# Key features made half by half, a changed warm-up, and weight stages at other key steps, in an attention and two-layer feed-forward kernel

## The chip, the cores and the metric

One core of a Trainium2 chip. The metric is device time in microseconds (us) of one execution, lower is better. The engines are TensorE (PE, with its weight loads as PEld), VectorE (DVE), ScalarE (ACT), GpSimd (POOL) and SyncE (SP, which issues DMAs here). Each works through its own queue in order.

## What is computed

Linear attention with random features over 4 batches, 8 heads, 576 positions and 64 dimensions, and then two feed-forward layers on the 2304 tokens (512 to 2048 and back):

```python
def phi(x):
    proj = np.einsum('bhsd,md->bhsm', x, omega)
    sq = np.sum(x * x, axis=-1, keepdims=True) / 2.0
    h = proj - sq
    h = h - np.max(h, axis=-1, keepdims=True)
    return np.exp(h) / np.sqrt(m)
q_p, k_p = (phi(q_s), phi(k_s))
kv = np.einsum('bhsm,bhsd->bhmd', k_p, v)
z = np.sum(k_p, axis=2)
...
g = np.maximum(h, 0.0) + alpha * np.minimum(h, 0.0)   # layer 1; layer 2 squares max(h, 0)
return (g @ w_out).astype(np.float32)
```

## The kernel before, in words

Every engine's order is the order in which the program is written out; a semaphore is waited for wherever an instruction uses what another engine has made. The work falls into three stretches: the keys (to about 57 us), the queries (to about 140 us), and the two feed-forward layers.

The keys come in 18 tiles of 128 tokens. `k_step(i)` (L656) issues, in this order: the load of a coming tile (SP), the products of key features and values of tile i-3 (`kv_part`, L644, PE), the projections of tile i (`project`, L598, 16 matmuls into one of two PSUM tiles of two banks), its square sums (`square_sums`, L605, into columns 0 to 7 of `tt[i % 2]`, a PSUM tile of one bank), and then for tile i-1 the maximum over features (`greatest`, L611, DVE), the bias made from it and the square sums (`bias`, L617 and L618, DVE), and the exponentials (`feature`, L623, ACT, eight activations). `kv_place` (L650, DVE) copies a finished batch out of PSUM. POOL copies values (L688) and squares the next tile (L587). Projections of tile i use the PSUM tile that the features of tile i-2 have read.

`idle(n)` (L589 to L592) issues n matmuls of zeros, 504 columns wide, into columns 8 to 511 of `tt[1]`; their results are not used. `ZEROS` gives how many stand ahead of the first projection, between the first projection and its square sums, and behind the square sums of tile 1.

Weights of the feed-forward layers are decoded and split beside this by `made()`, a generator; each `onward` does one stage. The first unit's stages 0 to 10 (L335 to L345) are: scale the first half's high words (ACT, L138); its low words (ACT, L143); shift it (DVE, L157) and scale the second half's high words; merge it (DVE L163, POOL L165) and the second's low words; shift the second; merge the second and cast (ACT, L244); remainder (DVE, L247); cast; remainder; two sums (DVE, L179); two sums. Stage 11 is empty for this unit. The loop at L771 runs one stage behind each key step from `MAKE_K` on, but none behind step `PLACED`; the two steps that follow run one each, and from query step 3 on `upto` counts stages.

The tiles `mx` and `nb` of a step come from a pool of four buffers.

Of the kernel before, what the change touches and what calls it, by code (L numbers as in the profile page):

```python
# [9 lines left out]
F32 = mybir.dt.float32  # L10
# [9 lines left out]
P = 128  # L20
B, H, S, D = 4, 8, 576, 64
T = B * S
NT = T // P
NP = H // 2
# [10 lines left out]
HB = NB // 2  # L35
NPAIR = NF // 2
QW = 2 * P
MAKE_K = 5

PLACED = 11  # L40

ZEROS = (8, 4, 4)

HELD = 5

# [16 lines left out]
def tile_performer_moe(ctx, tc, qt, kt, qn, kn, vn, omt, w1i, w1o, al, w2i, w2o, out):  # L62
    nc = tc.nc
# [378 lines left out]
    def onward(most, blk):  # L442

        ask(most, blk)
        next(making[0])
# [6 lines left out]
    def ask(most, blk):  # L452

        limit[0], room[0] = most, blk
        if not making:
            making.append(made())
            next(making[0])
        fetches[0]()
# [75 lines left out]
    def attention():  # L534
        with ExitStack() as ac:
# [3 lines left out]
            sm = ac.enter_context(tc.tile_pool(name="sm", bufs=4, side="right"))  # L539
# [8 lines left out]
            tt = [po.tile([P, 512], F32, name=f"t{j}") for j in range(2)]  # L548

            def projections(i):  # L550

                return (pb, pa)[i % 2].tile([P, 2, NP, M], F32, name="h")
# [23 lines left out]
            def load(key):  # L576
                which, i = key
                raws[key] = raw = ld.tile([P, NP, P], F32, name="raw")
                nc.sync.dma_start(out=raw, in_=(kt if which == "k" else qt)[i])

            def load_values(i):
                vls[i] = kp.tile([P, H, D], F32, name="vr", bufs=4)
                nc.sync.dma_start(out=vls[i], in_=vn[i * P:(i + 1) * P])

            def square(key):
                sqts[key] = wk.tile([P, NP, P], F32, name="sqt", bufs=2)
                nc.gpsimd.tensor_tensor(out=sqts[key], in0=raws[key], in1=raws[key], op=ALU.mult)  # L587

            def idle(n):  # L589

                for _ in range(n):
                    nc.tensor.matmul(tt[1][:, H:], zeros[:, 0:P], zeros[:, H:], start=True, stop=True)  # L592

            def project(key, pj):

                for c in range(NP):
                    for j, rows in enumerate(HALVES):
                        nc.tensor.matmul(pj[:, j, c, :], raws[key][rows, c, :], om[rows], start=True, stop=True)  # L598

            def square_sums(key, o):  # L600

                sqt = sqts.pop(key)
                for c in range(NP):
                    for rows in HALVES:
                        nc.tensor.matmul(o[rows, 2 * c:2 * c + 2], sqt[:, c, rows], pick,  # L605
                                         start=True, stop=True, skip_group_check=True)
                return o.rearrange("p (c j) -> p j c", j=2)

            def greatest(pj):
                mx = sm.tile([P, 2, NP], F32, name="mx")  # L610
                nc.vector.reduce_max(out=mx, in_=pj, axis=AX.X)  # L611
                return mx

            def bias(mx, nsq):

                nb = sm.tile([P, 2, NP], F32, name="nb")
                nc.vector.tensor_tensor(out=mx, in0=nsq, in1=mx, op=ALU.add)  # L617
                nc.vector.tensor_tensor(out=nb, in0=nsq, in1=mx, op=ALU.subtract)  # L618
                return nb

            def feature(pj, nb, e):
                for c in range(NP):
                    nc.scalar.activation(out=e[:, c, :], in_=pj[:, c, :], func=AF.Exp, bias=nb[:, c:c + 1])  # L623

            def parts_of(i):

                t0, out = i * P, []
                while t0 < (i + 1) * P:
                    t1 = min((i + 1) * P, (t0 // S + 1) * S)
                    out.append((t0 // S, slice(t0 - i * P, t1 - i * P), t0 % S == 0, t1 % S == 0))  # L630
                    t0 = t1
                return out


            pjs, nsqs, es, acc = {}, {}, {}, {}

            def kv_part(i, part):
                b, rs, first, last = part
                if first:
                    acc[b] = products()  # L640
                for h in range(H):
                    g, k = divmod(h, G)
                    for ms in HALVES:
                        nc.tensor.matmul(  # L644
                            acc[b][ms, g, k * W:(k + 1) * W], es[i][rs, h % 2, h // 2, ms], vas[i % 4][rs, h],
                            start=first and k == 0, stop=last, skip_group_check=True)

            def kv_place(b):
                o = acc.pop(b)
                nc.vector.tensor_copy(out=kvr[:, b].rearrange("p (g h) w -> p g (h w)", g=NG), in_=o[:, :, 0:G * W])  # L650
# [5 lines left out]
            def k_step(i):  # L656
                if 0 <= i < NT:
                    k = next(ahead, None)
                    if k:
                        load(k)  # L660
                    if i + 1 < NT:
                        load_values(i + 1)
                todo = parts_of(i - 3) if has(i - 3) else []
                placed = []
                if todo:
                    kv_part(i - 3, todo[0])
                    placed = [b for b, _, _, last in todo if last]
                if has(i):
                    pjs[i] = projections(i)
                    project(("k", i), pjs[i])  # L670
                    if i == 0:
                        idle(ZEROS[1])
                    nsqs[i] = square_sums(("k", i), tt[i % 2][:, 0:H])
                    if i == 1:
                        idle(ZEROS[2])
                if has(i - 1):
                    pj = pjs.pop(i - 1)
                    nb = bias(greatest(pj), nsqs.pop(i - 1))
                    es[i - 1] = e = kp.tile([P, 2, NP, M], F32, name="e", bufs=4)
                    feature(pj[:, 0], nb[:, 0], e[:, 0])  # L680
                for b in placed:
                    kv_place(b)
                if has(i - 1):
                    feature(pj[:, 1], nb[:, 1], e[:, 1])
                if len(todo) > 1:
                    kv_part(i - 3, todo[1])
                if has(i - 1):
                    nc.gpsimd.tensor_copy(out=vas[(i - 1) % 4][:, :, 0:D], in_=vls.pop(i - 1))  # L688
                if has(i + 1):
                    square(("k", i + 1))  # L690
                es.pop(i - 3, None)
# [4 lines left out]
            def q_step(s, make=lambda: None, more=lambda: None):  # L696
# [31 lines left out]
                if has(s):  # L728
                    qpj[s] = projections(s)
                    project(("q", s), qpj[s])  # L730
                    mx = greatest(qpj[s])
# [9 lines left out]
                if has(s):  # L741
                    nsq = square_sums(("q", s), tt[s % 2 if s < 2 else 1][:, 0:H])
                    qnb[s] = bias(mx, nsq)
# [13 lines left out]
            zeros = ka.tile([P, 512], mybir.dt.bfloat16, name="zeros")  # L757
            nc.vector.memset(zeros, 0.0)
            nc.vector.memset(warm, 0.0)
            for rows, queue in zip(HALVES, (nc.sync, nc.scalar)):  # L760
                queue.dma_start(out=om[rows], in_=omt)
            nc.scalar.activation(out=warm, in_=warm, func=AF.Exp)
            idle(ZEROS[0])
            load(next(ahead))
            load(next(ahead))
            k_step(-1)
            constants()
            nc.vector.tensor_scalar(out=om, in0=om, scalar1=scale, scalar2=None, op0=ALU.mult)
            load(next(ahead))
            load_values(0)  # L770
            for i in range(NT):  # L771
                k_step(i)
                if i == 1:
                    ask(1, BLOCKS - 1)
                elif i >= MAKE_K and i != PLACED:
                    onward(1, BLOCKS - 1)
                if i == 3:
                    gate[0] = 4
                    ask(1, BLOCKS - 1)
                if i == 2:  # L780
                    nc.sync.dma_start(out=al_sb, in_=al)
                if i == 8:
                    nc.vector.tensor_scalar(out=sg_sb, in0=al_sb, scalar1=1.0, scalar2=-2.0, op0=ALU.is_gt, op1=ALU.mult)
                    nc.vector.tensor_scalar(out=sg_sb, in0=sg_sb, scalar1=1.0, scalar2=None, op0=ALU.add)
                if i == NT - 1:
                    square(("q", 0))
# [272 lines left out]
    COMPLETE = {6: (0,), 7: (1, 2), 8: (3,), 9: (4, 5)}  # L1059

    attention()
    xp = ctx.enter_context(tc.tile_pool(name="xp", bufs=1, reuse_waits="tile"))
    for n in (T1, T2, T3):
# [23 lines left out]
    for n, (layer, k, turn, p) in enumerate(plan):  # L1087
# [12 lines left out]
        for m, got in enumerate(steps, DRAINED if n == 0 else 0):  # L1100
# [29 lines left out]
            for _ in range(FILL[0 if whole else 1][m]):  # L1130
                part, _ = next(fill, (None, None))
# [316 lines left out]
```

## Time and profile before

| | |
|---|---|
| median of 3 runs | 872.86 us (872.68 to 872.99) |
| the profiled execution | 872.57 us |
| its span | 870.8 us |
| PE busy | 865.3 us, 99% of the span |
| DVE busy | 676.0 us, 78% |
| ACT busy | 520.5 us, 60% |
| POOL busy | 96.8 us, 11% |

The span runs from the first instruction to the last; the rest of the execution's time lies around it. Matmuls are pipelined and their ends are modelled, so that PE's busy share overstates how close PE is to its limit; starts of matmuls and of weight loads are what to go by. In the rows below, a bracket at the end of a row is the idle time of that engine ahead of the row and what ended it.

### The profile page before, as it was taken

The numbers are of one execution on the slowest core, as the hardware profiler recorded it, in microseconds if no ns is written. First come the engines' busy times: TensorE is split into PE (matmuls) and PEld (weight loads), VectorE is DVE, ScalarE is ACT, GpSimd is POOL, SyncE is SP. The second block draws the span as 40 slices with busy tenths as digits, with TensorE's granted clock in tenths as the row PEclk, the third lists the DMA queues.
The fourth block names the chain that finished last, engine by engine and source line by source line (L and its number), as shares of the span: only waits on it lengthen the run. The fifth ranks groups of instructions, "written<-read, shape, count | busy, mean of one in ns | idle before, by whom it ended". The sixth has DMA issues, their size and how long they took to land.

```text
span 870.8 us, 17509 instructions
## 1 busy us (share of the span) xinstructions
PE 865.3 (99%) x6812; PEld 801.1 (92%) x6812; DVE 676.0 (78%) x1117; ACT 520.5 (60%) x1027; POOL 96.8 (11%) x138
## 2 busy tenths in 40 slices
PE   9999999999999999999999999999999999999998
PEld 7898889899999999989999999998899988999888
DVE  4778986998996776897877965669965699756686
ACT  5888886989876666577667733335423355333442
POOL 6652342111101000001000000000000000000000
PEclk9999999999999999999999999999999999999999
DMA  8545305899837999939999966777797686876774
GB/s 280 187 131 177 111 14 203 281 312 345 301 142 276 384 372 376 343 109 352 400 405 383 350 224 214 233 270 267 258 302 248 211 314 253 295 258 224 298 258 147
DMA packets 88530, 228.76 MB, mean 263 GB/s; under 512 B 6784, under 2 KB 19456, under 8 KB 83456
## 3 DMA queue, kind: packets, MB, share of 16 engines
q1 hardware_dynamic: 78880, 192.21, 61.5%
q0 software_dynamic: 9216, 33.56, 11.5%
q10 hardware_dynamic: 352, 1.87, 0.6%
q8 instruction: 54, 0.88, 0.4%
q14 instruction: 28, 0.23, 0.1%
HBM read 170.47 MB, written 57.15 MB: 261 GB/s over the span
## 4 chain that ended last, share of the span: by engine, by line
PE 97%; ACT 2%; issue 0%; DVE 0%; ACTq 0%
PE h L838 30%; PE y L1034 23%; PE sumc L1227 11%; PE spare L838 10%; PE suma L1227 9%; PE h L598 4%; PE o L644 2%; PE t L605 2%; PE t L718 2%; PE o L750 2%; PE t L737 1%; PE t L592 1%; ACT e L623 1%; PE h L1227 0%; ACT gh L863 0%
## 5 line engine op out<-in xcount | busy, mean ns | idle before, releaser
L838 PE MATMUL h<-xh,w 128*128 128x384 f32 x1016 | 286.3, 337 | 0.7 <-ACT s L863 0.4
L838 PEld LDWEIGHTS h<-xh,w 128*128 128x128 f32 x1016 | 186.3, 188 | 4.0 <-ACT s L863 0.7
L1034 PE MATMUL y<-gh,w 128*128 128x512 f32 (+1 forms) x768 | 174.0, 337 | 0.0
L838 PE MATMUL h<-xl,w 128*128 128x384 f32 x508 | 170.4, 335 | 0.0
L1034 PEld LDWEIGHTS y<-gh,w 128*128 128x128 f32 x768 | 130.8, 188 | 11.7
L1034 PE MATMUL y<-gl,w 128*128 128x512 f32 (+1 forms) x384 | 102.4, 337 | 0.0
L1242 ACT CAST gh<-g 128x768 fp32r<-128x768 f32 x72 | 56.9, 833 | 74.1 <-PE suma L1227 33.1
L838 PEld LDWEIGHTS h<-xl,w 128*128 128x128 f32 x508 | 95.5, 188 | 2.0
L838 PE MATMUL spare<-xh,w 128*128 128x384 f32 x336 | 91.4, 335 | 0.0
L1244 DVE TENSOR_TENSOR gl<-g,gh 128x768 fp32r<-128x768 f32 x72 | 65.7, 953 | 14.3 <-PE suma L1227 7.1
L1227 PE MATMUL sumc<-w,gh 128*128 128x512 f32 (+1 forms) x296 | 76.6, 379 | 0.0
L1034 PEld LDWEIGHTS y<-gl,w 128*128 128x128 f32 x384 | 67.1, 188 | 9.6
L838 PEld LDWEIGHTS spare<-xh,w 128*128 128x128 f32 x336 | 61.3, 188 | 0.5 <-DVE c L905 0.3
L1227 PEld LDWEIGHTS sumc<-w,gh 128*128 128x128 f32 x296 | 52.8, 189 | 9.3
L863 ACT ACTIVATE s<-h,sg_sb 128x384 f32<-128x384 f32 x66 | 38.1, 578 | 38.2 <-PE h L838 38.2
L611 DVE TENSOR_REDUCE mx<-h 128x8 f32<-128x1024 f32 x36 | 44.0, 1223 | 21.7 <-PE h L598 21.1
L881 DVE SCALAR_TENSOR_TENSOR c<-c,al_sb 128x768 f32<-128x768 f32 x48 | 49.2, 1025 | 10.2 <-ACT c L863 10.2
L838 PE MATMUL spare<-xl,w 128*128 128x384 f32 x168 | 56.2, 334 | 0.0
L876 DVE SCALAR_TENSOR_TENSOR c<-h,sg_sb,s 128x384 f32<-128x384 f32 x66 | 40.5, 614 | 18.3 <-PE h L838 7.2
L1227 PE MATMUL suma<-w,gh 128*128 128x512 f32 x216 | 52.4, 391 | 0.0
L1227 PE MATMUL sumc<-w,gl 128*128 128x256 f32 x280 | 48.5, 282 | 0.0
L887 DVE SCALAR_TENSOR_TENSOR gl<-c,sg_sb,gh 128x768 fp32r<-128x768 f32 x48 | 48.4, 1009 | 0.0
(133 smaller groups left out, 1484.7 us busy)
## 6 DMA issues: line engine op xcount, KB each, us to landing
w<-k SPq DMA_DIRECT2D x99, 512.0 KB, 5.2
w<-k SPq DMA_DIRECT2D x39, 1024.0 KB, 4.8
w<-k SPq DMA_DIRECT2D x26, 896.0 KB, 8.8
k<-ms SPq DMA_DIRECT2D x36, 512.0 KB, 7.7
k<-w SPq DMA_DIRECT2D x16, 512.0 KB, 6.2
x<-in_w2i POOLq DMA_DIRECT2D x16, 512.0 KB, 7.0
x<-in_w2o POOLq DMA_DIRECT2D x16, 512.0 KB, 7.2
ms<-in_w1o POOLq DMA_DIRECT2D x14, 512.0 KB, 5.7
```

The lines of the kernel that those rows point to most:

```text
L598: nc.tensor.matmul(pj[:, j, c, :], raws[key][rows, c, :], om[rows], start=True, stop=True)
L605: nc.tensor.matmul(o[rows, 2 * c:2 * c + 2], sqt[:, c, rows], pick, start=True, stop=True, skip_group_check=True)
L611: nc.vector.reduce_max(out=mx, in_=pj, axis=AX.X)
L838: nc.tensor.matmul(out, w[:, u, a, cs], tiles[v, b][:, kc], start=start and kc == 0 and j == 0, stop=stop and kc == 1 and j == 2, skip_gro ...
L863: nc.scalar.mul(out=to, in_=of, mul=sg_sb[:, 2 * p + i:2 * p + i + 1])
L876: nc.vector.scalar_tensor_tensor(out=c[:, ts], in0=b, scalar=sign, in1=s, op0=ALU.mult, op1=ALU.add)
L881: nc.vector.scalar_tensor_tensor(out=c, in0=c, scalar=slope, in1=c, op0=ALU.mult, op1=ALU.max)
L887: nc.vector.scalar_tensor_tensor(out=gl[:, i], in0=c, scalar=sign, in1=gh[:, i].bitcast(F32), op0=ALU.mult, op1=ALU.subtract)
L1034: nc.tensor.matmul(y[a0 // 512][:, a0 % 512:a0 % 512 + a1 - a0], u[:, i, c * P:(c + 1) * P], v[:, i, ts], start=first and j == 0 and a0 % ...
L1227: nc.tensor.matmul(to[c] if v == 3 or banks else to[c][:, :QW], (l if v == 2 else h)[:, r, c * P:(c + 1) * P], both(r) if v == 3 else w[:, ...
L1242: nc.scalar.copy(out=h[:, r], in_=f[:, r])
L1244: nc.vector.tensor_tensor(out=l[:, r], in0=f[:, r], in1=h[:, r].bitcast(F32), op=ALU.subtract)
```

## The change

Three things. `greatest` and `bias` are called once for each half of a key tile (4 of its 8 groups of 128 features), so that the order on DVE is maximum, two bias instructions, maximum, two bias instructions; `mx` and `nb` come from the same pool of four. The zeros between the first projection and its square sums are gone, and those behind the square sums of tile 1 are five instead of four and are written to `tt[0]` instead of `tt[1]`. And the first unit's twelve stages behind the key loop's steps run at the steps of a table.

```diff
-MAKE_K = 5
-
-PLACED = 11
-
-ZEROS = (8, 4, 4)
+MAKE_K = {5: 1, 7: 1, 9: 1, 10: 1, 12: 2, 13: 1, 14: 1, 15: 1, 16: 1, 17: 2}
+
+ZEROS = 8, 5
...
-            def idle(n):
+            def idle(n, j=1):
 
                 for _ in range(n):
-                    nc.tensor.matmul(tt[1][:, H:], zeros[:, 0:P], zeros[:, H:], start=True, stop=True)
+                    nc.tensor.matmul(tt[j][:, H:], zeros[:, 0:P], zeros[:, H:], start=True, stop=True)
...
-            def greatest(pj):
-                mx = sm.tile([P, 2, NP], F32, name="mx")
+            def greatest(pj, n=2):
+                mx = sm.tile([P, 2, NP], F32, name="mx")[:, :n]
                 nc.vector.reduce_max(out=mx, in_=pj, axis=AX.X)
                 return mx
 
-            def bias(mx, nsq):
-
-                nb = sm.tile([P, 2, NP], F32, name="nb")
+            def bias(mx, nsq, n=2):
+
+                nb = sm.tile([P, 2, NP], F32, name="nb")[:, :n]
...
                     project(("k", i), pjs[i])
-                    if i == 0:
-                        idle(ZEROS[1])
                     nsqs[i] = square_sums(("k", i), tt[i % 2][:, 0:H])
                     if i == 1:
-                        idle(ZEROS[2])
+                        idle(ZEROS[1], 0)
                 if has(i - 1):
                     pj = pjs.pop(i - 1)
-                    nb = bias(greatest(pj), nsqs.pop(i - 1))
                     es[i - 1] = e = kp.tile([P, 2, NP, M], F32, name="e", bufs=4)
-                    feature(pj[:, 0], nb[:, 0], e[:, 0])
+                    nsq = nsqs.pop(i - 1)
+                    nb = [bias(greatest(pj[:, j:j + 1], 1), nsq[:, j:j + 1], 1)[:, 0] for j in range(2)]
+                    feature(pj[:, 0], nb[0], e[:, 0])
                 for b in placed:
                     kv_place(b)
                 if has(i - 1):
-                    feature(pj[:, 1], nb[:, 1], e[:, 1])
+                    feature(pj[:, 1], nb[1], e[:, 1])
...
-                elif i >= MAKE_K and i != PLACED:
+                for _ in range(MAKE_K.get(i, 0)):
                     onward(1, BLOCKS - 1)
```

## Rows read from the trace of the kernel before

**Rows 1.** The page, busy time of each engine over the span, share, instructions.
```profile
PE 865.3 (99%) x6812; PEld 801.1 (92%) x6812; DVE 676.0 (78%) x1117; ACT 520.5 (60%) x1027; POOL 96.8 (11%) x138
```
**Rows 2.** The chain that ended last, 0 to 75 us: start, length, engine, line.
```profile
1.20 3.54 PE t L592 x8
4.73 1.55 PE h L598 x16
...
14.35 0.56 PE t L605 x16
14.91 0.99 PE o L644 x32
15.90 1.09 PE h L598 x16
...
36.89 2.18 ACT e L623 x8
```
**Rows 3.** The opening in order of time: start, length, engine, line, operation, tiles.
```profile
5.95 1.04 POOL L587 TENSOR_TENSOR sqt<-raw 128x512 f32<-128x512 f32 x1
...
7.86 0.17 DVE L617 TENSOR_TENSOR mx<-t,mx 128x8 f32<-128x8 f32 x1 [0.29 <-PE t L605]
...
8.06 0.17 DVE L618 TENSOR_TENSOR nb<-t,mx 128x8 f32<-128x8 f32 x1
...
8.32 2.17 ACT L623 ACTIVATE e<-h,nb 128x128 f32<-128x128 f32 x8 [5.45 <-DVE nb L618]
...
8.83 0.63 PE L605 MATMUL t<-pick,sqt 128*64 128x2 f32 x16
...
8.95 1.23 DVE L611 TENSOR_REDUCE mx<-h 128x8 f32<-128x1024 f32 x1 [0.72 <-PE h L598]
...
9.40 1.02 PE L592 MATMUL t<-zeros 128*128 128x504 bf16 x4
...
10.46 0.17 DVE L617 TENSOR_TENSOR mx<-t,mx 128x8 f32<-128x8 f32 x1 [0.28 <-PE t L592]
10.54 0.97 PEld L598 LDWEIGHTS h<-om,raw 64*128 64x128 f32 x16 [0.61 <-ACT e L623]
```
**Rows 4.** The same view, steady key steps.
```profile
15.83 1.16 PE L598 MATMUL h<-om,raw 64*128 64x128 f32 x16
...
17.04 1.22 DVE L611 TENSOR_REDUCE mx<-h 128x8 f32<-128x1024 f32 x1 [0.94 <-PE h L598]
...
18.64 0.17 DVE L618 TENSOR_TENSOR nb<-t,mx 128x8 f32<-128x8 f32 x1
...
18.90 2.17 ACT L623 ACTIVATE e<-h,nb 128x128 f32<-128x128 f32 x8 [0.54 <-DVE nb L618]
```
**Rows 5.** The same view, around the features that the chain names at 36.89.
```profile
36.10 0.97 PEld L598 LDWEIGHTS h<-om,raw 64*128 64x128 f32 x16
...
36.40 0.17 DVE L617 TENSOR_TENSOR mx<-t,mx 128x8 f32<-128x8 f32 x1 [0.51 <-PE o L644]
...
39.11 0.97 PEld L598 LDWEIGHTS h<-om,raw 64*128 64x128 f32 x16 [0.44 <-ACT e L623]
```
**Rows 6.** Groups by line and shape, 9 to 57 us: busy us, mean ns, idle before.
```profile
L611 DVE TENSOR_REDUCE mx<-h 128x8 f32<-128x1024 f32 x17 | 20.8, 1222 | 10.9 <-PE h L598 10.9
...
L650 DVE COPY kvr<-o 128x520 f32<-128x520 f32 x3 | 2.1, 689 | 0.0
...
L247 DVE TENSOR_TENSOR w<-wf,w 128x512 fp32r<-128x512 f32 x2 | 2.1, 1026 | 0.2 <-ACT w L244 0.2
...
L163 DVE SCALAR_TENSOR_TENSOR x<-x,t 128x512 int32<-128x512 int32 x2 | 1.4, 680 | 0.0
...
L157 DVE TENSOR_SCALAR t<-x 128x512 int32<-128x512 int32 x2 | 0.8, 421 | 0.0
```
**Rows 7.** Busy by stretch at the span's end: PE, PEld, DVE, ACT, POOL, granted clock.
```profile
869.00:870.80 1.80, 0.00 (x0) 0.00 (x0) 0.00 (x0) 0.00 (x0) 0.00 (x0) 1.00 0.21 73
```
**Rows 8.** Waits of PE, 56 to 165 us: total, times, longest.
```profile
PE h L838 <- ACT c L863: 0.3, 1, 0.3
```

## The prediction

> **What bounds the kernel now.** I read the engines' busy times first, then the chain that ended last, then the opening in order of time, then the groups by line. TensorE (PE) is busy for 99% of the span [rows 1]; as its ends are modelled, I don't take that for a bound by itself. The chain says more: from the third projection to 75 us it runs on PE, in steps of projection (1.09 us), square sums (0.56) and keys-times-values (0.99), 2.64 us together, and leaves PE at one long place, 36.89, for 2.18 us of ScalarE (ACT) features; in the opening the features of tile 0, at 8.32, hold up the third projection in the same way [rows 3]. So a key step is bound by PE, and what can be won in these steps is PE's waiting: 0.6 us ahead of the third projection (weight loads idle 0.61 at 10.54) [rows 3], and 0.37 us at 39.11 (39.11 less 36.10 is 3.01, a step is 2.64) [rows 5]. From 56 to 165 us PE waits for another engine once, 0.3 us [rows 8]. So what the key steps gain or lose moves everything behind them by the same amount; nothing later gives it back, as the later work is ordered behind it on the same engine.
>
> **How tight a step is.** A projection goes into one of two PSUM tiles, so projection i waits for the features of i-2. In the steady rows [rows 4]: projection at 15.83, maximum (L611) at 17.04, ACT at 18.90 and its features over 2.17 later, at 21.07. That loop is 5.24 us, with 0.05 to PE again 5.29, against two steps of PE, 5.28. VectorE (DVE) needs 17.04 to 18.64 and most of L618's 0.17, of which the next start overlaps a part (I count 0.08): 1.68 us of each 2.64.
>
> **Part 1: the opening.** Removed: the four zero matmuls between projection 0 and its square sums, about 1 us of PE (four take 1.02) [rows 3]. Projection 0 ends at 6.28 (4.73 and 1.55) [rows 2]. The square sums of 0 then end at 6.85; POOL squares tile 1 from 5.95 to 6.99 [rows 3], so the squares of 0 are done by then and tile 1 has landed. Projection 1 ends at 7.94, square sums 1 at 8.50. Five zeros follow; at 1.02 for four they take about 1.24 and end at 9.7.
>
> What matters is where these five write: tt[0], the tile in which the square sums of key tile 0 lie, and they come in program order ahead of bias 0, which reads those. In the kernel before, the zeros behind square sums 1 wrote tt[1], and the row of bias 1 (L617, 10.46) shows what that does: the maximum of 1 ended at 10.18, square sums 1 at 9.46, and still L617 started only 0.04 us behind the last zero matmul (9.40 and 1.02 give 10.42), which the row names as releaser [rows 3]. The columns are disjoint, the wait is there all the same. Bias 0, reading tt[0], has no such row: its L617 at 7.86 waited for the square sums alone. After the change the two change places: bias 1 is free of the zeros, and bias 0 gets them. Before, the wait cost 0.28 us of DVE, under cover of ACT's features of 0. Bias 0 has no cover: nothing else feeds ACT yet.
>
> Worked out: L617 at 9.74, L618 0.20 behind (7.86 to 8.06), ACT 0.26 behind that (8.06 to 8.32) [rows 3]: features begin at 10.20. Queued behind the waiting L617 on DVE is the second half's maximum: it begins 0.08 after L618, at 10.02, takes 0.69 (below), L617 and L618 follow, and the second four activations can begin at about 11.27; four take 1.17 (2.17 less four of 0.25), to 12.43, and 0.05 later projection 2 runs: 12.48 against 10.54, **+1.93** (+1.8 to +2.1 with the half maximum and the fifth zero at their bounds). PE waits from 9.7 to 12.5.
>
> **Part 2: halves.** No row shows a maximum over 512. The whole, 1024 values, takes 1.222; a DVE copy of 520 values out of PSUM takes 0.689, which puts a value at 1.06 ns and the fixed part at 0.14 us; half of the whole would be 0.61 [rows 6]. I take 0.69, as the copy is the same engine reading as many values from the same memory; bounds 0.61 and 0.72. The Trainium skill ("VectorE: DVE Perf Modes", section on the TRN2 errata) gives a PSUM-source instruction a fixed 120 cycles plus one per value at 0.96 GHz; an estimate from that page is 0.66, and 1.19 for the whole, where the trace has 1.22, so I keep the row's figure; by the page's the shortage below would be about a third smaller.
>
> One half then costs DVE 0.69, something from there to L618, and 0.08 to the next start. From the maximum's end to L618 it is 0.38 in the steady row (17.04 and 1.22 to 18.64) [rows 4]; L617 to L618 alone is 0.20 [rows 3]. I take 0.31, between them and nearer the steady row, as the second half has no square sums left to wait for. A step takes 2.17 (1.94 to 2.30), where it took 1.68. What it buys: ACT begins after one half, 1.25 instead of 1.86 us behind the projection, but the second half's bias gates the second four activations, so features end about 3.49 behind and the loop, with 1.21 ahead of the maximum and 0.05 behind the features, is 4.75, 0.53 shorter than two steps of PE. That lead removes no PE wait where there was none; it can cover one.
>
> **Part 3: weight stages.** The twelve stages that ran at key steps 5 to 10 and 12 to 17 run at 5, 7, 9, 10, 12 (two), 13 to 16 and 17 (two, the second empty). All are done by the same step, so the query steps keep theirs. No weight DMA moves: both transfers of the first unit are issued at steps 1 and 3, and SP's queue of key loads is passed by nothing. POOL's two merges (L165, an addition of the size of a squaring, 1.04) [rows 3] go from steps 8 and 10 to 10 and 12, in front of a copy and a squaring there; a tile is squared in the step before the one that uses it, so that 1.04 is under cover of most of a step's 2.64: nothing, and 1.04 at the worst, once a merge. ACT has one scaling or cast in a step at most, and 2.17 of features in 2.64; what it lacks it borrows from the lead.
>
> DVE is what runs short. Step 11 has the copy of kvr (0.69, so 0.61 to the next start), step 12 now has shift and merge (0.42 and 0.68, so 0.34 and 0.60), step 13 the remainder L247 (1.03, so 0.95) [rows 6]: with three steps of 2.17 that is 9.01, against 7.92 of PE. 1.09 too much, less the lead of 0.53: PE waits 0.56 at projection 14. Steps 14 to 17 hold 8.68, another remainder (0.85), a kvr copy and four sums (0.5 each by half a remainder, as they have half its elements, 1.8 in all with their overlap), 11.9 against PE's 11.7 (4 steps of 2.64 and 1.1 for the tile whose keys-times-values is issued in two parts), and ACT's cast at 14 finds the lead spent: about 0.35 more. **+0.9**; at 0.61 for a half it is 0, at 2.30 a step 0.13 more in each of seven, 1.8.
>
> The wait at 36.40 (L617 held 0.5 us, though what it reads was ready) cost PE 0.37 because the loop had no lead; step 11 is left with one: **-0.37** (0 if DVE's shortage meets it).
>
> **Sum.** 1.93 + 0.9 - 0.37 = 2.46 us on the profiled execution, 872.57 (span 870.8 and 1.77 around it): 875.03. The median of the runs is 0.29 above that execution: **875.3**.
>
> **Rivals.**
> *The zeros don't hold bias 0* (not slower). Then L617 follows the first half's maximum at 7.13, ACT begins at 7.59, its second half at 8.66, projection 2 runs at 9.87, 0.67 earlier than before; with +0.9 and -0.37 that is -0.14: 872.7. It decides at one point, whether the first L617 starts near 7.1 or near 9.7. For it: the columns are disjoint. Against it: the row of bias 1. Chance 0.10.
>
> *DVE doesn't run short.* With a half at 0.61 the shortage is covered by the lead: 1.93 - 0.37 = 1.56, 874.4. For it: the maximum may have no fixed part to speak of; against it the copies. Chance 0.12.
>
> *TensorE's clock falls in the new wait of 2.8 us.* The first eight zeros took 3.54 us, 0.44 each, against 0.25 in the later four, and projection 0 took 1.55 against 1.09 [rows 2, 3]: the lower of the two levels, 1.2 GHz, early on. One key step at the first pace instead of the second, 2.64 times 0.44 over 0.25, costs 2.0: 877.3. At the end of the span PE does nothing for at least 1.8 us and the granted clock stays at 1.00 [rows 7], which speaks against, though the new wait is longer. The Trainium skill ("TensorE: Matmul & The Clock Gate", section "Why this matters for your kernels") says that PE-idle gaps between bursts bring the clock down to half; the trace has no gap so long between bursts. Chance 0.14.
>
> *Faster by over 0.2%.* No hold and no shortage together give -0.67 - 0.37, 871.8; for less than 871.1 another 0.7 would have to come from a wait that these views don't show. Chance 0.02.
>
> **How the numbers follow.** The forecast has 0.62. About 0.2% (1.75 us, so 874.6) is what a measurement of this kernel can tell from no change. Slower: 0.55 of the forecast's 0.62, 0.03 of the second rival, 0.14: 0.72. Same: 0.07, 0.09 and the first rival's 0.10, together 0.26. Faster 0.02. The range 873.8 to 877.6 holds the forecast with its bounds (874.0 to 876.6), the second rival and over half of the clock's; it leaves out the first and the last.
>
> **What would show it.** Right: the first L617 at 9.7 released by L592, projection 2 at 12.5, DVE back to back over key steps 11 to 15 with PE waiting for features at projections 14 and 15. Wrong: L617 at 7.1; no wait of PE behind 36 us; key-step matmuls at half speed behind 12.5.

## The result, and the profile after

The changed kernel took 879.55 us (median of 9 runs, 878.97 to 882.53) and the kernel before, beside it, 872.68 (872.30 to 879.21). The ratio is 1.0077, 95% interval 1.0063 to 1.0091: slower by 6.9 us, where 2.4 were forecast, and outside the stated range, whose upper end was 877.6. The profiled execution of the changed kernel is the one at 882.53, its slowest, with a span of 880.8; a second profile of the same kernel (below, span 877.1, 878.88 us) is nearer to the median. The kernel before has some slow runs of its own, 7 of the 83 beside the experiments, at 875.4 to 879.2 us with a granted clock of 0.992 to 0.996 over the whole run, and they widen the intervals below.

The page after: span, busy times as in [rows 1], and TensorE's granted clock in 40 slices of 22 us, in tenths.

```profile
span 880.8 us, 17576 instructions
PE 871.0 (99%) x6809; PEld 807.1 (92%) x6809; DVE 682.2 (77%) x1171; ACT 520.8 (59%) x1027; POOL 97.1 (11%) x138
PEclk7899999999999999999999999999999999999999
```

PE is still "99% busy"; the line that tells is the clock, below full in the first two slices. The opening in order of time, as in [rows 3] (L590 is the zeros, L609 the maximum, L615 and L616 the bias, L621 the features, L596 the projection):

```profile
6.16 1.16 PE L596 MATMUL h<-om,raw 64*128 64x128 f32 x16
...
7.82 1.24 PE L590 MATMUL t<-zeros 128*128 128x504 bf16 x5
...
9.09 0.16 DVE L615 TENSOR_TENSOR mx<-t,mx 128x4 f32<-128x4 f32 x1 [2.69 <-PE t L590]
9.29 0.16 DVE L616 TENSOR_TENSOR nb<-t,mx 128x4 f32<-128x4 f32 x1
9.37 0.68 DVE L609 TENSOR_REDUCE mx<-h 128x4 f32<-128x512 f32 x1
...
10.15 4.25 ACT L621 ACTIVATE e<-h,nb 128x128 f32<-128x128 f32 x16 [7.27 <-DVE mx L609]
...
12.38 2.08 PE L596 MATMUL h<-om,raw 64*128 64x128 f32 x16 [3.32 <-ACT e L621]
...
17.17 2.08 PE L596 MATMUL h<-om,raw 64*128 64x128 f32 x16
```

Bias 0 waits for the five zeros, as forecast: 2.69 us of DVE, released by L590. ACT then starts not behind the first half's bias (9.29 and 0.16) but 0.10 us behind the end of the second half's maximum (9.37 and 0.68), which the row names. PE waits 3.32 us, and its projections then take 2.08 us and stand 4.79 us apart (12.38 to 17.17), not 1.16 as in [rows 4] and 2.64. From the start of projection 1 (6.16) to that of projection 2 it is 6.22 us; before, it was 2.81 (7.74 to 10.55). Busy time by stretch, columns as in [rows 7]:

```profile
5.00:10.00 5.00, 4.05 (x65) 2.94 (x63) 1.57 (x4) 0.00 (x0) 4.68 (x12) 1.00 1.03 377
10.00:15.00 5.00, 2.62 (x28) 2.40 (x30) 2.70 (x10) 4.25 (x16) 1.66 (x3) 0.61 0.81 286
15.00:20.00 5.00, 5.00 (x72) 4.66 (x72) 2.12 (x7) 2.18 (x8) 2.20 (x3) 0.50 0.57 177
20.00:25.00 5.00, 5.00 (x72) 4.66 (x73) 1.94 (x6) 2.18 (x8) 1.59 (x2) 0.50 0.41 140
25.00:30.00 5.00, 5.00 (x96) 4.75 (x96) 2.40 (x9) 2.73 (x9) 2.31 (x3) 0.68 0.48 114
```

The clock is at its lower level, 1.2 GHz (0.50), for three key steps and part of a fourth, with PE busy throughout. In the first 5 us of a span the column can't be used in this way: there it reads 1.00 in every profile, while the first eight zeros take some 0.44 us each [rows 2] and the five at 7.82 take 0.25; the pace tells. Behind the low stretch the clock is full, and DVE is what PE waits for by way of ACT:

```profile
51.65 1.17 DVE L245 TENSOR_TENSOR w<-wf,w 128x512 fp32r<-128x512 f32 x1
52.73 0.68 DVE L609 TENSOR_REDUCE mx<-h 128x4 f32<-128x512 f32 x1
...
53.61 1.16 PE L596 MATMUL h<-om,raw 64*128 64x128 f32 x16 [0.54 <-ACT e L621]
...
54.59 2.18 ACT L621 ACTIVATE e<-h,nb 128x128 f32<-128x128 f32 x8 [1.03 <-DVE mx L609]
...
56.82 1.16 PE L596 MATMUL h<-om,raw 64*128 64x128 f32 x16 [0.50 <-ACT e L621]
```

These two are projections 14 and 15.

Where the 10.0 us of span went, by the starts of projections in the two profiles. To projection 2: 12.38 against 10.55, +1.8. From there to projection 6: 30.06 less 12.38 is 17.68, against 21.12 less 10.55, +7.1 (the clock). From 6 to the first query tile: 66.02 less 30.06 is 35.96, against 56.23 less 21.12, +0.85 (DVE). The rest to the end, 814.8 against 814.6: +0.2. In the profile nearer to the median the same four are +2.3, +2.9, +0.85 and +0.2, 6.3 in all. The third of these is too small by a halt in the profile of before, which the prediction passed over: projection 6 takes 1.67 us there instead of 1.16, and the idle in it ends on nothing that the profile shows ("issue").

```profile
21.12 1.67 PE L598 MATMUL h<-om,raw 64*128 64x128 f32 x16
...
22.19 0.41 PEld L598 LDWEIGHTS h<-om,raw 64*128 64x128 f32 x5 [0.33 <-issue]
```

Without that 0.5 us, before would take 34.60 from projection 6 to the first query tile, and the change 1.36 more.

### The profile page after: what moved, and what is told of

It reads as the page before. It is cut to its first block, busy times and chain, and to the rows that moved or that the text cites. A ratio compares the mean times of both kernels' runs of the same rounds, so it can differ in the third digit from the quotient of the medians.

```text
span 880.8 us, 17576 instructions
## 1 busy us (share of the span) xinstructions
PE 871.0 (99%) x6809; PEld 807.1 (92%) x6809; DVE 682.2 (77%) x1171; ACT 520.8 (59%) x1027; POOL 97.1 (11%) x138
## 4 chain that ended last, share of the span: by engine, by line
PE 93%; ACT 3%; DVE 2%; issue 1%; DMA 0%; POOL 0%; DVEq 0%; ACTq 0%
PE h L835 28%; PE y L1031 22%; PE sumc L1224 11%; PE spare L835 10%; PE suma L1224 9%; PE h L596 4%; PE t L715 2%; PE t L603 2%; PE o L642 2%; PE o L747 2%; PE t L734 1%; DVE mx L609 1%; PE t L590 1%; ACT e L621 0%; DMA ms<-in_w1i 0%
## 5 line engine op out<-in xcount | busy, mean ns | idle before, releaser
L609 DVE TENSOR_REDUCE mx<-h 128x4 f32<-128x512 f32 (+1 forms) x54 | 46.7, 864 | 20.3 <-PE h L596 19.3
L621 ACT ACTIVATE e<-h,nb 128x128 f32<-128x128 f32 x144 | 39.2, 391 | 23.6 <-DVE mx L609 23.5
L596 PE MATMUL h<-om,raw 64*128 64x128 f32 x576 | 45.2, 300 | 4.6 <-ACT e L621 4.4
```

## The experiments

The kernel before took 872.77 us beside the first four runs, 872.58 beside the next four, 872.50 beside the last three; "above before" is against the one beside it. Two theories stood at the start. The first: the zeros in tt[0] hold bias 0, PE falls idle, and the clock falls with that. The rival: there are too few zeros, or the halves and the stages are what costs.

### The zeros back in the other tile

```diff
-                        idle(ZEROS[1], 0)
+                        idle(ZEROS[1], 1)
```

> The changed kernel with its five zeros written to tt[1] again; all else as changed. Theory (the wait and the clock): bias 0 no longer waits for the zeros, so ScalarE's first features start near 8.2 us instead of 10.15, projection 2 near 10.4 instead of 12.4, and the granted clock stays at 1.00 behind that. What is left is VectorE's shortage in the key steps, about 1.3 us net of the two small waits of before: 873.7. Rival (the number of zeros: 13 instead of 16, none between the projections, are too few to hold the clock, wherever they are written): the clock falls all the same, and the time stays at 878 or more.

873.63 us, 0.9 above before and 0.1 from the expectation; the interval of the ratio (0.9993 to 1.0019) takes in no change. The number of zeros is as changed. The chain of this run, and the line of PE's waits from 0 to 165 us:

```profile
8.40 2.18 ACT e L621 x8
10.62 1.16 PE h L596 x16
...
PE h L596 <- ACT e L621: 1.8, 3, 0.7
```

Features of tile 0 start at 8.40, projection 2 is at 10.62, and the granted clock is 1.00 throughout. So six of the seven microseconds hang on the tile that the zeros are written to, and the rival's first half falls. What is left is 1.8 us of PE's waits for features.

### The wait kept, PE kept at work

```diff
                         idle(ZEROS[1], 0)
+                        idle(10, 1)
```

> The changed kernel with ten more zero matmuls to tt[1] behind its five to tt[0], so that TensorE works through most of the wait for bias 0, which stays. Theory: the wait keeps its own price, 1.8 us at projection 2 (about 12.4 us), but the clock stays at 1.00: 872.7 + 1.8 + 1.3 = 875.8. If the wait alone, or the halves and the stages, cost what was lost, the time stays near 879.5.

876.46 us, 3.7 above before (expected 875.8), 3 below the changed kernel. In order of time, and by stretch:

```profile
8.01 3.36 PE L590 MATMUL t<-zeros 128*128 128x504 bf16 x15
...
12.56 1.16 PE L596 MATMUL h<-om,raw 64*128 64x128 f32 x16 [1.19 <-ACT e L621]
...
10.00:15.00 5.00, 3.81 (x69) 2.74 (x69) 3.42 (x13) 4.29 (x16) 2.95 (x5) 1.00 0.82 289
```

Projection 2 comes no earlier, at 12.56 (6.21 behind projection 1, as in the change), but PE was idle for 1.19 us only, and the clock stays at 1.00. The wait and the clock are two prices.

### The zeros' change alone, with and without PE at work

The kernel before, with no zeros between the first projections and five to tt[0] behind square sums 1:

```diff
-ZEROS = (8, 4, 4)
+ZEROS = (8, 0, 5)
...
-                        idle(ZEROS[2])
+                        idle(ZEROS[2], 0)
```

> The kernel before with the change of the zeros alone (none between the first two projections, five to tt[0] behind the square sums of tile 1); maxima whole, stages as before. Theory: bias 0 waits for the zeros, features start near 9.5 us, projection 2 near 11.8 instead of 10.5 (+1.2), TensorE idle some 2.8 us; with the clock falling 4 to 7 more, 878 to 880, without 873.9. If the time is near 873.9, the halves' part of the idle (the second maximum that lies between bias and features) is what takes the clock down. Rival (halves and stages are the cost): 872.7.

876.31 us, 3.5 above before: between the two values, as the wait came out larger (projection 2 at 12.55 instead of 11.8) and the clock's part smaller. The whole maximum of tile 0 runs ahead of the wait here, and projection 2 stands 5.62 us behind projection 1, 0.6 less than with the halves.

The same with eight more zeros to tt[1] behind them, which shortens PE's idle (and holds bias 1 by 0.2 us, under cover of ACT's features of tile 0):

```diff
                         idle(ZEROS[2], 0)
+                        idle(8, 1)
```

> The kernel with the zeros' change alone (e3_zeros_alone, 3.5 us above the kernel before) with eight more zero matmuls to tt[1] behind the five, so that TensorE's idle in the opening is 1 us instead of 2.7. Theory: the wait for bias 0 stays (projection 2 near 12.3, +1.9), the clock holds: 874.6. If it stays near 876.3, the wait costs more than its own 1.9 without the clock.

874.02 us, 1.5 above before. First the projection and the stretches of the run with PE idle, then those of the run with PE at work:

```profile
12.55 0.81 PE L598 MATMUL h<-om,raw 64*128 64x128 f32 x6 [2.73 <-ACT e L623]
...
10.00:15.00 5.00, 2.45 (x28) 2.22 (x30) 2.18 (x6) 4.23 (x16) 2.11 (x3) 0.78 0.85 302
15.00:20.00 5.00, 5.00 (x78) 4.66 (x78) 1.76 (x4) 2.17 (x8) 2.19 (x3) 0.54 0.58 199
```

```profile
12.54 1.16 PE L598 MATMUL h<-om,raw 64*128 64x128 f32 x16 [1.03 <-ACT e L623]
...
10.00:15.00 5.00, 3.97 (x70) 2.83 (x69) 2.86 (x6) 4.25 (x16) 2.39 (x4) 1.00 0.88 297
```

Projection 2 starts within 0.01 us of the same time in both; 2.73 us of idle goes with a fall of the clock, 1.03 without. The wait by itself costs 1.5 us. The fall costs 2.0 by what each run stands above its own before, and 2.3 by the two medians (876.31 less 874.02), which are from two chips.

### The stages alone, the halves alone

The stage table in the kernel before:

```diff
-MAKE_K = 5
+MAKE_K = {5: 1, 7: 1, 9: 1, 10: 1, 12: 2, 13: 1, 14: 1, 15: 1, 16: 1, 17: 2}
...
-                elif i >= MAKE_K and i != PLACED:
+                for _ in range(MAKE_K.get(i, 0)):
```

> The kernel before with the change of the stages alone. Theory: VectorE takes 1.7 of each 2.64 us with whole maxima, so the double stage at step 12 fits but for about 0.1 us: 872.5 to 873.1. Rival (the stage table costs by itself, through its double steps): 873.7 or more.

872.31 us, 0.5 below before, ratio 0.9987 (0.9969 to 1.0005): no difference that can be told. By themselves the stages cost nothing that the times show.

The halves in the kernel before, zeros and stages as they were:

```diff
...
-                    nb = bias(greatest(pj), nsqs.pop(i - 1))
+                    nsq = nsqs.pop(i - 1)
+                    nb = [bias(greatest(pj[:, j:j + 1], 1), nsq[:, j:j + 1], 1)[:, 0] for j in range(2)]
...
```

> The kernel before with the halves alone (zeros and stages as before). Theory: the halves take VectorE's slack (near 2.2 of each 2.64 us instead of 1.7) and win nothing, since ScalarE's first features wait for the second half's maximum too; TensorE waits for features in the key steps with weight stages: +0.8, 873.5, the clock at 1.00. Rival (the halves shorten the loop as meant): 872.3 or less.

873.77 us, 1.2 above before, by medians; the interval of the ratio (0.9990 to 1.0021) takes in no change, so this is a measured direction and not a settled size. The clock stays at 1.00. The halves alone win nothing.

### Two PSUM tiles for a projection

With the zeros in tt[1]. A projection gets two tiles of one bank, so that one half's features and the other half's maximum no longer meet in one tile:

```diff
-                return (pb, pa)[i % 2].tile([P, 2, NP, M], F32, name="h")
+                return [(pb, pa)[i % 2].tile([P, NP, M], F32, name=f"h{j}") for j in range(2)]
...
```

> The changed kernel with its zeros to tt[1] (as e1_zeros_other_bank) and with each projection in two PSUM tiles of one bank instead of one of two banks. Theory (the wait of the first features for the second half's maximum comes from both lying in one tile): features of tile 0 start near 7.6 instead of 8.4 us, projection 2 near 9.9 instead of 10.6, and the loop of a key step gets 0.6 us of lead, so that TensorE's waits for features shrink: 872.3. Rival (VectorE's own work is the bound, the lead is used up as well): the waits at projections 12 to 15 stay and only the opening is won, 873.0; or features still start behind the second maximum, 873.6.

872.36 us: 0.2 below before (ratio 0.9991, 0.9975 to 1.0007, which takes in no change), 1.3 below the same with one tile by medians, and 0.1 from the expectation.

```profile
7.77 0.16 DVE L617 TENSOR_TENSOR nb<-t,mx 128x4 f32<-128x4 f32 x1
7.85 0.68 DVE L610 TENSOR_REDUCE mx<-h 128x4 f32<-128x512 f32 x1
8.03 2.18 ACT L622 ACTIVATE e<-h,nb 128x128 f32<-128x128 f32 x8 [5.17 <-DVE nb L617]
...
10.06 1.35 PE L596 MATMUL h<-om,raw 64*128 64x128 f32 x16
...
46.42 1.73 PE L596 MATMUL h<-om,raw 64*128 64x128 f32 x16
...
46.99 0.96 PEld L596 LDWEIGHTS h<-om,raw 64*128 64x128 f32 x14 [0.28 <-ACT e L622]
```

ACT now starts 0.26 us behind the start of the first half's bias (L617), in the middle of the second half's maximum, released by nb and no longer by the maximum. PE's matmuls have no listed wait for features in the key steps any more, but its weight loads have one, inside projection 15 (46.99), and the steps from projections 14 and 15 still take 2.95 and 3.30 us instead of 2.64. The start at 8.03 settles what held the first features in the changed kernel: the second half's maximum reads the same PSUM tile, and ACT's reads of the other bank are made to wait for it.

### No zeros behind the square sums of tile 1

> The changed kernel without any zeros behind the square sums of tile 1. Bias 0 then waits for its square sums alone, and TensorE has nothing to do from about 8.4 to 10.4 us. Theory: an idle of 2 us, where the changed kernel has 3.3 and the one with the zeros alone 2.7, is short enough in most runs; the clock stays and the time is that of e1_zeros_other_bank, 873.6. If the clock falls here too: 876 or more.

876.39 us, 3.8 above before: a miss. Bias 0 waits for nothing, features start at 7.80 and projection 2 is at 10.03, earlier than before, and yet:

```profile
10.03 1.16 PE L596 MATMUL h<-om,raw 64*128 64x128 f32 x16 [1.91 <-ACT e L621]
...
10.00:15.00 5.00, 4.97 (x78) 4.73 (x80) 2.08 (x7) 3.89 (x16) 3.85 (x6) 0.67 0.90 311
...
10.00:11.00 1.00, 0.97 (x16) 0.97 (x16) 0.14 (x1) 1.00 (x5) 1.00 (x2) 1.00 1.13 340
11.00:12.00 1.00, 1.00 (x28) 0.89 (x26) 0.69 (x1) 1.00 (x5) 0.75 (x3) 0.83 0.60 207
12.00:13.00 1.00, 1.00 (x24) 1.00 (x22) 0.87 (x3) 0.04 (x1) 1.00 (x2) 0.50 0.91 317
```

An idle of 1.91 us came before a fall here, and the fall came when PE had been at work again for over a microsecond. All ten runs show a granted clock below 1.00 (0.990 to 0.998). So the zeros do matter, as work for PE, and the wait isn't needed for the fall. Whether they matter because they shorten the idle or because they are more work isn't separated: zeros change both.

### Zeros and halves without the stages, and the change again

> The changed kernel with the stages at the steps of before. Theory: the stages have no part in the loss; the halves make the idle in the opening 0.6 us longer than with the zeros alone and with it the fall of the clock longer: near 879.5, within 0.7. If the stages are a part of what is lost beyond the zeros alone (876.3): 877 to 878.5.

878.18 us (ten runs, 876.98 to 882.48), 5.6 above before.

> The changed kernel as it is, timed beside the next two on one chip. With the stages of before it took 878.2 on another chip, in its own record 879.55. If the stages add to the loss, through the low clock or VectorE: near 879.5 again. If they don't and the difference was the chip's: near 878.2.

879.05 us, 6.6 above before. The change and the change without its stages differ by 0.9, on two chips with a spread of 4.1 and 5.5 us, so the times alone don't settle what the stages add; the table below compares the key steps. Stretches of the change's second profile:

```profile
10.00:15.00 5.00, 2.13 (x18) 1.91 (x20) 2.71 (x10) 4.25 (x16) 2.14 (x3) 0.72 0.91 308
15.00:20.00 5.00, 5.00 (x84) 4.76 (x86) 2.41 (x7) 2.18 (x8) 2.19 (x3) 0.59 0.53 144
20.00:25.00 5.00, 4.99 (x122) 4.54 (x121) 3.52 (x13) 3.08 (x12) 3.18 (x4) 1.00 0.70 216
```

Here the clock is back by 20 us, where the first profile, 3.6 us slower, still shows 0.50 from 20 to 25. The time lost to the clock varies from run to run with that.

### Halves in the opening alone

Two tiles and zeros in tt[1] as above, halves for key tiles 0 and 1, and one bias from two maxima from tile 2 on:

```diff
+                    if i - 1 < 2:
+                        nb = [bias(greatest(pj[j:j + 1], 1), nsq[:, j:j + 1], 1)[:, 0] for j in range(2)]
+                    else:
+                        both = bias(greatest(pj), nsq)
...
```

> As e6_two_tiles (two PSUM tiles for a projection, zeros to tt[1]), but with halves for key tiles 0 and 1 alone; from tile 2 on there are two maxima and one bias, so that VectorE takes near 1.8 of each 2.64 us. Theory (halves pay in the opening, where nothing else feeds ScalarE, and cost VectorE's time behind it): projection 2 near 10.0 and no wait for features behind it: 872.0, 0.3 to 0.7 below the kernel before and e6_two_tiles no faster. Rival (halves are worth their lead in every step): e6_two_tiles, at 0.2 below the kernel before, is the better.

872.00 us, 0.5 below before, ratio 0.9994 (0.9985 to 1.0004). Projection 2 is at 9.83, as expected, but the interval takes in no change, and it can't be told from the two-tile version with halves throughout. The profiled execution took 873.58 us and has a halt in projection 6 as before has, a longer one:

```profile
22.46 0.60 PE L596 MATMUL h<-om,raw 64*128 64x128 f32 x5 [0.88 <-issue]
```

No version was found that beats the kernel before by more than the measurement tells.

### What the starts of the projections say of all kernels

From the profiles, in us: the start of projection 2, the time from the start of projection 1 to it, the time from projection 2 to projection 6 (where the clock shows), and from projection 6 to the first query tile's projection (where DVE shows).

| kernel | projection 2 | 1 to 2 | 2 to 6 | 6 to the first query tile |
|---|---|---|---|---|
| before | 10.55 | 2.81 | 10.57 | 35.11 |
| the change, first profile | 12.38 | 6.22 | 17.68 | 35.96 |
| the change, second profile | 12.87 | 6.22 | 13.46 | 35.96 |
| zeros in the other tile | 10.62 | 3.62 | 10.72 | 35.97 |
| wait kept, PE at work | 12.56 | 6.21 | 10.72 | 35.96 |
| no zeros behind | 10.03 | 3.64 | 12.21 | 36.00 |
| zeros and halves, stages of before | 13.59 | 6.21 | 13.73 | 35.06 |
| halves alone | 11.27 | 3.40 | 10.73 | 34.98 |
| stages alone | 10.10 | 2.80 | 10.58 | 35.17 |
| zeros alone | 12.55 | 5.62 | 13.65 | 34.45 |
| zeros alone, PE at work | 12.54 | 5.63 | 10.58 | 34.62 |
| two tiles (halves and stages) | 10.06 | 2.82 | 10.76 | 35.36 |
| two tiles, halves in the opening alone | 9.83 | 2.83 | 10.81 | 36.48 |

The start of projection 2 moves with the length of projection 0, which differs from execution to execution (1.16 us in the change's first profile, 2.08 with two tiles). The second column is free of that; for before it is read from these rows:

```profile
7.74 1.16 PE L598 MATMUL h<-om,raw 64*128 64x128 f32 x16
...
10.55 1.16 PE L598 MATMUL h<-om,raw 64*128 64x128 f32 x16
```

It is 2.80 or 2.81 without the wait and without halves, 3.40 to 3.64 with halves in one tile and no wait, 5.62 or 5.63 with the wait and no halves, and 6.21 or 6.22 wherever the halves stand behind the wait. So the halves themselves put off projection 2 by 0.6 to 0.8 us, as ACT's first features wait for the second half's maximum, and with two tiles (2.82) they don't. Against before, the change has 3.41 more here, less the 1.0 or so that the four removed zeros took ahead of projection 1: a net loss of 2.4.

The third column is 10.6 to 10.8 where PE was idle for less than 1.2 us ahead of it, and 12.2 to 17.7 where it was idle for 1.9 or more.

In the last column two rows have to be read without their halts in projection 6: 0.5 in before, 1.3 in the last row. Then it is 34.45 to 34.62 with neither halves nor stages, 35.17 with the stages alone (with 0.15 of such a halt), 34.98 and 35.06 with the halves and the stages of before, 35.96 to 36.00 with both in one tile, 35.36 with both in two tiles, and 35.2 with halves in the opening alone. So either costs about 0.4 us in the key steps, and the two together 1.4, or 0.8 with two tiles.

## Why the prediction was wrong

The direction and the first mechanism were right, the size was not. The step that failed is the clock's: the forecast's sum put it at nothing and left it to a rival of chance 0.14, which took it to last one key step; it took 2.9 us in the profile nearer to the median and 7.1 in the other. A second step was wrong beside it, that ACT begins after one half; it made two terms of the sum too small.

**The wait of bias 0** was read rightly from one row of before, the L617 at 10.46 that waited for zeros in columns it doesn't read [rows 3]. After: L615 at 9.09, released by L590. The sum's +1.93 measured +1.8 and +2.3 in the two profiles, and 2.4 when the length of projection 0 is taken out. From bias 0 to projection 2 it took 3.29 us (9.09 to 12.38), where 2.74 were worked out (9.74 to 12.48). That the first profile comes so near to +1.93 is luck, two errors that cancelled: the zeros ended at 9.06 instead of 9.7, since projection 0 took 1.16 us there instead of 1.55, and the features started later than worked out.

**ACT begins after one half** was wrong. The loop was given 0.53 us of lead by that; it got none, since ACT's first features wait for the second half's maximum in the same PSUM tile (10.15 after; 8.03 with two tiles). The row at 10.46 had shown that dependences here go by more than the columns used; I applied it to the zeros and not to the halves. The price of a half (0.69) was right, 0.68.

**DVE's shortage** was right in kind and place, and too small. PE waits for features at projections 14 and 15, the two named, and the steps that end there take 3.24 and 3.21 us instead of 2.64: 1.2 us, where 0.9 was worked out with a lead that ACT never had. Smaller losses in other steps come with the halves alone, and the sum had none of them. Net of before's waits the sum had 0.53 for the key steps; the profiles have 0.85, or 1.36 without before's halt in projection 6. The 0.90 between the change and the same without its stages (35.96 less 35.06) hits the +0.9 by chance, as the 35.06 holds losses of the halves that the working doesn't have.

**The clock** is the failed step. I took PE's 1.8 idle microseconds at a granted 1.00 in [rows 7] as speaking against a fall. PE had in fact been idle for 3.1 us when the span ended there. But the row ends with the span, and a fall can come later than the idle: with no zeros behind square sums 1 it came when PE had been at work again for over a microsecond. So the row shows that an idle can pass without a fall, not that the next one will. In the runs an idle of 1.03 and 1.19 us held the clock, while 1.91, 2.73 and 3.32 lost it; where the limit lies, and what else decides it, they don't show. The price of one key step at the lower clock was right: 2.0, where 4.79 less 2.64 is 2.15. How many there are was not: in whole or in part, two steps ran at 1.2 GHz with the zeros alone, four in the change's first profile and two in its second. That is 2.0 to 2.3 us in time with the zeros alone, and 7.1 and 2.9 from projection 2 to 6 in the change. The Trainium skill ("TensorE: Matmul & The Clock Gate", section "Why this matters for your kernels"), cited for the rival, has the right direction: a gap between bursts took the clock down.

In the second profile, 2.3 for the wait, 2.9 for the clock, 0.85 for the key steps and 0.2 behind them make 6.3, of the 6.6 to 6.9 that the medians give; the sum had 1.93, nothing, 0.53 and nothing.

**What the parts do together** is more than their sum by medians: 3.5 (zeros), 1.2 (halves) and -0.5 (stages) give 4.2, not 6.6. Of the 2.4 that are missing, about 0.6 is what halves and stages lose in the key steps only when they stand together (1.36 less 0.4 and 0.4). The 0.6 of the halves ahead of projection 2 is in both sums. The rest was not separated: behind the wait the halves also make PE's idle longer (3.32 us against 2.73), and what the low clock costs differs between executions of one kernel. Why the low stretch is twice as long in some runs (882.5 us) as in others stays open too, and so does one run without the stages, 881.71 us, whose granted clock is 1.00.

## What to carry to other kernels

A filler matmul is a writer like any other: put it into a tile that nobody on the critical path reads next, and look for a row in which an instruction waited for columns that it doesn't use. Splitting a reduction in halves buys latency only if the halves lie in different tiles, and it costs the engine its slack in every step, so it belongs where that engine isn't near its limit. Price an idle of PE twice, once as time and once as a fall of the clock behind it; the second was the larger here (2.9 against 2.3 us in the second profile).

## What the runs showed of the hardware that I had not expected

TensorE's granted clock fell to 0.50 behind an idle of 1.91 us, when PE had been at work again for over a microsecond. Once down, it stayed there with PE busy for 5.00 of 5.00 us, for up to three key steps and part of a fourth. Ten or eight matmuls on zeros, whose results nobody reads, put into the idle time held it at 1.00 in all ten runs of each kernel, and were worth 2.0 to 2.3 us with the zeros' change alone and about 3 with the whole change (879.05 to 879.55, and 876.46).
